# One list-scheduled order for all engines, PSUM banks by class, batch 0 mixed pair by pair, and the tails of all batches as a ninth MLP block

## The chip, the cores and the metric

One core of a Trainium2 chip. The metric is the time of one execution on the device, in microseconds (us), as the median of several runs. A run is called fast or slow by its time and its granted matrix-engine clock. PE is the matrix engine (PEld its weight loads), ACT the scalar engine, DVE the vector engine, POOL the GpSimd engine, SP the sync engine, which here only issues DMAs. POOL issues the loads that also cast from f32 to bf16; SP issues plain loads, stores and DMA transposes.

## The reference

Random-feature attention for 8 batches of 8 heads, then a mixer. In short:

```python
def _attn_ref(q, k, v, omega):              # q, k, v: 8 x 8 x 576 x 64, omega: 128 x 64
    phi = lambda x: concat(cos(x @ omega.T), sin(x @ omega.T)) / sqrt(128)
    kv  = einsum('bhsm,bhsd->bhmd', phi(k), v)
    z   = sum(phi(k), axis=2)
    num = einsum('bhsm,bhmd->bhsd', phi(q), kv)
    den = einsum('bhsm,bhm->bhs', phi(q), z)     # kept away from 0
    return num / den

def _moe_ref(x, U, V, w_ch1, w_ch2):        # x: 8 x 576 x 512, w_ch1: 512 x 2048, w_ch2: 2048 x 512
    h = x.transpose(0, 2, 1) @ U @ V        # token mixing of rank 32
    u = x + h.transpose(0, 2, 1)
    return u + maximum(u @ w_ch1, 0) @ w_ch2
```

The kernel works by head pair (32 of them, four to a batch). A *quad* is the k, q and v of four heads, so two quads to a batch: quads 0 and 1 are batch 0, quads 2 and 3 batch 1. Of a batch's 576 tokens 512 make four full tiles; the other 64 are its *tail*. In the code and the traces kraw and qraw are a quad's k and q as loaded, kT and qT their transposes; x is the attention's result, u the token-mixed x, and uT its transpose, which the MLP's first matmuls (W1, from w_ch1) read; W2 is w_ch2. *Mixing* is the way from x to u.

## The kernel before

It lets a framework schedule instructions written in a loop of steps: in step `s` one quarter of an MLP block (two batches behind), the angles of head pair `s` and the attention of pair `s - 1`. All matmul outputs share two rotating sets of PSUM buffers, `"at"` and `"mm"`.

```python
    def angles(g):                                   # head pair g
        pk = psum.tile([P, 2, 512], F32, name="pk", tag="at")
        ...                                          # 8 matmuls, then DVE scales to int32 "ang"
        for a in range(2):
            nc.scalar.activation(out=ft[:, 0, a, :], in_=low[:, a, :, 0], func=ACT.Sin, scale=TO_RAD)
            nc.gpsimd.tensor_scalar(out=ang[:, a, :], in0=ang[:, a, :], scalar1=TURN / 4.0,
                                    scalar2=1.0, op0=ALU.add, op1=ALU.mult)      # a quarter turn: cosine next
        for a in range(2):
            nc.scalar.activation(out=ft[:, 1, a, :], in_=low[:, a, :, 0], func=ACT.Sin, scale=TO_RAD)
    ...
    def channel_in(b, fs):                           # W1 groups of batch b
        for f0 in fs[::2]:
            h_ps = psum.tile([P, 2, SM], F32, name="h_ps", tag="mm")
            for f in range(2):
                for ct in range(NCT):
                    nc.tensor.matmul(h_ps[:, f, :], w1(ct, f0 + f), uT[:, :, ct, :],
                                     start=(ct == 0), stop=(ct == NCT - 1))
                nc.scalar.activation(out=hid[:, f0 + f, :], in_=h_ps[:, f, :], func=ACT.Relu)
    ...                                              # channel_in_tail: after every second batch, 64 matmuls of 128 columns
    for s in range(NG + 6):
        if s >= 6:
            b, mc = divmod(s - 6, 4)
            if b < B:
                mlp_chunk(b, mc)
        n = s // 2 + 1
        if s % 2 == 0 and 4 <= n < NG // 2:
            load_quad(n); load_v(n); transpose_quad(n); widen_v(n)
        ...
        if s < NG:
            angles(s)
        ...                                          # weights: W1 from step 3 on, W2 in steps 4 and 5
        if s != 4:
            attend(s - 1)
```

Of the kernel before, what the change touches and what calls it, by code (L numbers as in the profile page):

```python
# [30 lines left out]
HALF = M * 9  # L31


# [3 lines left out]

# [3 lines left out]


SYNC = mybir.DependencyInfo(mybir.DependencyClass.Sync, mybir.DependencyReason.DATA)
# [3 lines left out]
def kernel(  # L47
# [23 lines left out]
    hidp = ctx.enter_context(tc.tile_pool(name="hidp", bufs=1))  # L71
    outp = ctx.enter_context(tc.tile_pool(name="outp", bufs=3))
    smallp = ctx.enter_context(tc.tile_pool(name="smallp", bufs=4))
    psum = ctx.enter_context(tc.tile_pool(name="psum", bufs=2, space=bass.MemoryType.PSUM))


    ident = const.tile([P, P], BF16, name="ident")
    om_f = stage.tile([P, 2, D], F32, name="om_f")
    nc.sync.dma_start(om_f, omega.unsqueeze(1).to_broadcast([P, 2, D]))
    warm = stage.tile([P, 1], F32, name="warm")  # L80
    nc.vector.memset(warm, 0.0)
    nc.scalar.activation(out=warm, in_=warm, func=ACT.Sin)
    WT = const.tile([P, M], BF16, name="WT")

    def omega_t():
        om_b = stage.tile([P, 2, D], BF16, name="om_b")
        nc.vector.tensor_copy(om_b, om_f)
        wt_ps = psum.tile([P, P], BF16, name="wt_ps", tag="at")
        nc.tensor.transpose(wt_ps, om_b, ident)
        nc.vector.tensor_copy(WT, wt_ps)  # L90

# [3 lines left out]
    U_f = stage.tile([P, NT + 1, R], F32, name="U_f")  # L95
    Vf = stage.tile([P, S], F32, name="Vf")

    def load_low_rank():
        U9 = moe_U.rearrange("(p s) r -> p s r", s=NS)
        for g in range(4):  # L100
            ordered(nc.sync.dma_start(Vf[g * R:(g + 1) * R, :], moe_V))
        for e in range(2):
            r = slice(e * TL, (e + 1) * TL)
            ordered(nc.sync.dma_start(U_f[r, 0:NT, :], U9[:, e:2 * NT:2, :]))
            ordered(nc.sync.dma_start(U_f[r, NT, :], U9[:, 8, :]))

    def cast_low_rank():
        ordered(nc.gpsimd.tensor_copy(Ub, U_f[:, 0:NT, :]))
        ordered(nc.gpsimd.tensor_copy(Ut, U_f[:, NT, :]))
        ordered(nc.gpsimd.tensor_copy(Vb.rearrange("r (s p) -> r s p", p=TL), Vf.rearrange("r (p s) -> r s p", s=NS)))  # L110

    W1b = const.tile([P, 4, NCT, 512], BF16, name="W1b")
    W2b = const.tile([P, NFT, C], BF16, name="W2b")

    def load_w1(a):
        return nc.gpsimd.dma_start(W1b[:, a, :, :],
                                   moe_w_ch1[:, a * 512:(a + 1) * 512].rearrange("(c p) f -> p c f", p=P))

    def load_w2(a):
        return nc.gpsimd.dma_start(W2b[:, 4 * a:4 * a + 4, :],  # L120
                                   moe_w_ch2[a * 512:(a + 1) * 512, :].rearrange("(f p) c -> p f c", p=P))

    def w1(ct, f):
        return W1b[:, f // 4, ct, f % 4 * P:(f % 4 + 1) * P]

    NV = 4
    vq = []
    for i in range(NV):
        a = const.tile([P, 2 * NS, D + 1], BF16, name=f"vq{i}")
        nc.vector.memset(a[:, :, D:D + 1], 1.0)  # L130
        vq.append(a)

    def ordered(ins):
        return tc.keep_in_program_order(ins)


    raw, tpos = {}, {}
# [5 lines left out]
    def load_quad(n, parts=1):  # L143
        for name in ("k", "q"):
            raw[name, n] = rawp.tile([P, 2, NS * D], BF16, name=f"{name}raw")
        for i in range(parts):
            w = slice(i * 2 // parts, (i + 1) * 2 // parts)
            for name, src in (("k", k), ("q", q)):
                last = ordered(nc.gpsimd.dma_start(raw[name, n][:, w, :], quad(src, n)[:, w, :]))
        return last  # L150

    def load_v(n):
        raw["v", n] = rawp.tile([P, 2, NS * D], F32, name="vraw")
        return ordered(nc.sync.dma_start(raw["v", n], quad(v, n)))

    def widen_v(n):
        ordered(nc.gpsimd.tensor_copy(vq[n % NV][:, :, 0:D],
                                      raw.pop(("v", n)).rearrange("p i (s d) -> p (i s) d", d=D)))

    def transpose_quad(n):  # L160
        for name in ("k", "q"):
            tpos[name, n] = tposp.tile([P, NS, P], BF16, name=f"{name}T")
            last = ordered(nc.sync.dma_start_transpose(tpos[name, n], raw.pop((name, n)).rearrange("p i e -> p (i e)")))  # L163
        return last

    def transpose_first():
        for name in ("k", "q"):
            tpos[name, 0] = tposp.tile([P, NS, P], BF16, name=f"{name}T")
        for blocks in (range(0, 4), range(4, NS)):
            t_ps = psum.tile([P, 2, 8, P], BF16, name="t_ps", tag="mm")  # L170
            for j, (name, copy) in enumerate((("k", nc.vector.tensor_copy), ("q", nc.scalar.copy))):
                src = raw[name, 0].rearrange("p i e -> p (i e)")
                for c in blocks:
                    nc.tensor.transpose(t_ps[:, j, c - blocks[0], :], src[:, c * P:(c + 1) * P], ident)
                copy(out=tpos[name, 0][:, blocks[0]:blocks[-1] + 1, :], in_=t_ps[:, j, 0:len(blocks), :])


    st, x_of = {}, {}

    def angles(g):  # L180
        n, i = divmod(g, 2)
        kT, qT = tpos["k", n], tpos["q", n]

        ang = angp.tile([P, 2, HALF], I32, name="ang")

        def units(dst, src):
            nc.vector.tensor_scalar(out=dst, in0=src, scalar1=TO_UNITS, scalar2=None, op0=ALU.mult)  # L187

        def at(s):
            f = NS * i + s  # L190
            return slice((f % 2) * D, (f % 2 + 1) * D), f // 2

        pk = psum.tile([P, 2, 512], F32, name="pk", tag="at")
        for j in range(4):
            for e in range(2):
                r, c = at(2 * j + e)
                nc.tensor.matmul(pk[:, e, j * P:(j + 1) * P], kT[r, c, :], WT[r, :])  # L197
        units(ang[:, 0, 0:1024], pk.rearrange("p e c -> p (e c)"))
        pt = psum.tile([P, 2, M], F32, name="pt", tag="at")
        r, c = at(8)  # L200
        nc.tensor.matmul(pt[:, 0, :], kT[r, c, :], WT[r, :])
        nc.tensor.matmul(pt[:, 1, :], WT[r, :], qT[r, c, :])  # L202
        units(ang.rearrange("p a c -> p (a c)")[:, 1024:1280], pt.rearrange("p a c -> p (a c)"))
        pq = psum.tile([P, 2, 512], F32, name="pq", tag="at")
        for e in range(2):
            r, c = at(e)
            nc.tensor.matmul(pq[:, e, :], WT[r, :], qT[r, c:c + 4, :])  # L207
        units(ang[:, 1, P:HALF].rearrange("m (t e p) -> m e t p", e=2, p=TL),
              pq.rearrange("m e (t p) -> m e t p", p=TL))

        ft = featp.tile([P, 2, 2, HALF], BF16, name="ft")
        low = ang.rearrange("p a c -> p (a c)").bitcast(I16).rearrange(
            "p (a c e) -> p a c e", a=2, e=2)
        for a in range(2):
            nc.scalar.activation(out=ft[:, 0, a, :], in_=low[:, a, :, 0], func=ACT.Sin, scale=TO_RAD)  # L215
            nc.gpsimd.tensor_scalar(out=ang[:, a, :], in0=ang[:, a, :], scalar1=TURN / 4.0,  # L216
                                    scalar2=1.0, op0=ALU.add, op1=ALU.mult)
        for a in range(2):
            nc.scalar.activation(out=ft[:, 1, a, :], in_=low[:, a, :, 0], func=ACT.Sin, scale=TO_RAD)  # L219
        st[g] = ft  # L220

    def key_values(g):
        n, i = divmod(g, 2)
        ft = st[g]
        kv_ps = psum.tile([P, 2, 512], F32, name="kv_ps", tag="mm" if g < 4 else "at")
        for f in range(2):
            o = slice(f * (D + 1), (f + 1) * (D + 1))
            for s in range(NS):
                c = (s % 2 * 4 + s // 2) * M if s < 8 else 1024
                for hh in range(2):  # L230
                    r = slice(hh * TL, (hh + 1) * TL)
                    nc.tensor.matmul(kv_ps[:, hh, o], ft[r, f, 0, c:c + M], vq[n % NV][r, NS * i + s, :],  # L232
                                     start=(s == 0), stop=(s == NS - 1))
        kvb = kvp.tile([P, 2, 2, D + 1], BF16, name="kvb")
        nc.vector.tensor_copy(kvb.rearrange("p h f d -> p h (f d)"), kv_ps[:, :, 0:2 * (D + 1)])  # L235
        st[g] = (ft, kvb)

    def numerators(g):
        b, hp = divmod(g, 4)
        ft, kvb = st.pop(g)  # L240
        if hp == 0:
            x_of[b] = xp.tile([P, NT, C], BF16, name="x")
            if b % 2 == 0:
# [139 lines left out]
    def mlp_chunk(b, mc):  # L383
# [4 lines left out]
        elif mc == 2:  # L388
            channel_out(b, (0, 1))
            if b % 2 == 1:  # L390
                channel_in_tail(b // 2)
# [102 lines left out]
```

## Time and profile before

| | before |
|---|---|
| median of 3 runs | 428.71 us (428.13 to 429.35) |
| profiled span | 426.5 us |
| PE busy | 363.9 us, 85% |
| first W1 matmul | 47.2 us |
| a pair of batches in the middle | 98.0 and 96.4 us |

Of the profile page of the kernel before, the span, PE's busy line, and the rows of 40 equal slices (10.66 us each; a digit is tenths busy, or tenths of full clock):

```profile
span 426.5 us, 8510 instructions
...
PE 363.9 (85%) x3639; PEld 186.5 (44%) x3639; DVE 198.4 (47%) x335; ACT 226.3 (53%) x278; POOL 122.9 (29%) x131
...
PE   3364988978899979978899989978899989979995
...
PEclk9996899999999999989999999999999999999999
DMA  8989998578247581677439483498438320133013
```

PE is lightly used in the first four slices and shows a rhythm of dips after that. The DMA engines are near full only for some 80 us.

The same page, three of the costliest groups (line, engine, operation, out<-in, shapes, count | busy us, mean ns | idle before it, and what ended it):

```profile
L339 PE MATMUL h_ps<-uT,W1b 128*128 128x512 bf16 x512 | 122.6, 379 | 14.3 <-ACT hid L341 12.8
L364 PE MATMUL ch_ps<-W2b,hid 128*128 128x512 bf16 x512 | 123.3, 383 | 5.1 <-DVE o L367 3.9
L254 PE MATMUL nd<-kvb,ft 128*128 128x65 bf16 x512 | 23.0, 198 | 7.5 <-DVE kvb L235 7.2
```

W1 groups wait 12.8 us in all for ACT's relu to free their buffer. In the page's chain of waits PE has just over half:

```profile
PE 53%; ACT 19%; DVE 9%; POOL 7%; issue 6%; DMA 3%; SPq 2%; POOLq 0%; ACTq 0%; DVEq 0%
```

Busy time by stretch (stretch, its length, then busy us of each engine with counts, granted clock, DMA share of 16 engines, GB/s). A share adds up the packets' times, so packets in flight together can bring it over 1:

```profile
0.00:40.00 40.00, 18.48 (x303) 13.51 (x303) 20.57 (x41) 22.89 (x23) 22.36 (x31) 0.94 0.93 169
40.00:80.00 40.00, 34.26 (x336) 16.66 (x337) 21.78 (x37) 25.22 (x33) 19.14 (x21) 0.93 1.03 176
80.00:115.00 35.00, 29.96 (x308) 14.55 (x306) 18.82 (x31) 20.65 (x25) 10.54 (x10) 1.00 0.64 128
115.00:380.00 265.00, 242.46 (x2471) 122.66 (x2471) 131.31 (x219) 145.57 (x180) 70.89 (x69) 0.99 0.52 97
101.60:199.60 98.00, 89.36 (x900) 44.80 (x900) 48.84 (x82) 55.61 (x69) 28.48 (x29) 0.98 0.57 110
199.60:296.00 96.40, 87.68 (x901) 44.37 (x900) 48.87 (x82) 55.57 (x69) 28.44 (x28) 1.00 0.63 111
```

One line of PE's timeline gives the true price of a matmul: 64 of them in a row, no gap.

```profile
385.39 14.06 PE L339 MATMUL h_ps<-uT,W1b 128*128 128x512 bf16 x64
```

The group's mean is 379 ns, but a start comes every 217 ns (13.89 us of the chain for 64). Records overlap, so work is counted in starts.

### The profile page before, as it was taken

Reading aid. Unit: us, or ns where it says so; the run is one execution under the profiler, and the core shown is the slowest. Engines: PE = TensorE matmul, PEld = TensorE weight load, DVE = VectorE, ACT = ScalarE, POOL = GpSimd, SP = SyncE. Lnnn points to the kernel's source line nnn. Section 1 sums busy time; section 2 is a strip of 40 time slices with the busy share of each in tenths; the row PEclk is TensorE's granted clock in tenths of the full one; section 3 lists DMA queues with packets and bytes.
Section 4 is the critical chain, followed back from the end, with each engine's and each line's share of the span. In section 5 each row is a group of like instructions: output and inputs, shape, how many; then the busy total and the mean of one; then the engine's idle time right before and its main releaser. Section 6 shows DMA issues by size and latency. Waiting matters only on the chain.

```text
span 426.5 us, 8510 instructions
## 1 busy us (share of the span) xinstructions
PE 363.9 (85%) x3639; PEld 186.5 (44%) x3639; DVE 198.4 (47%) x335; ACT 226.3 (53%) x278; POOL 122.9 (29%) x131
## 2 busy tenths in 40 slices
PE   3364988978899979978899989978899989979995
PEld 2253444434455434434456444434456444434452
DVE  2566663564535643664435552674434561550011
ACT  2667598327835196626845197626855187405320
POOL 5366583123323060423232051424233031200000
PEclk9996899999999999989999999999999999999999
DMA  8989998578247581677439483498438320133013
GB/s 134 180 172 208 192 192 146 106 178 170 36 81 137 120 155 18 111 172 155 59 56 162 84 170 39 81 174 174 68 40 178 75 50 2 26 70 68 9 41 74
DMA packets 76533, 46.54 MB, mean 109 GB/s; under 512 B 55376, under 2 KB 67664, under 8 KB 76496
## 3 DMA queue, kind: packets, MB, share of 16 engines
q1 hardware_dynamic: 63536, 32.37, 36.6%
q0 software_dynamic: 12960, 13.63, 21.2%
q8 instruction: 28, 0.46, 0.5%
q14 instruction: 9, 0.07, 0.0%
HBM read 37.14 MB, written 9.44 MB: 109 GB/s over the span
## 4 chain that ended last, share of the span: by engine, by line
PE 53%; ACT 19%; DVE 9%; POOL 7%; issue 6%; DMA 3%; SPq 2%; POOLq 0%; ACTq 0%; DVEq 0%
PE ch_ps L364 23%; PE h_ps L339 15%; ACT ft L215 7%; ACT ft L219 7%; POOL ang L216 6%; DVE ang L187 4%; ACT hid L341 4%; PE ch_ps L376 3%; PE ht_ps L352 3%; PE nd L254 2%; SPq L163 2%; DVE u L313 2%; DMA kraw<-in_k_dram 1%; PE hn L312 1%; DMA vraw<-in_v_dram 1%
## 5 line engine op out<-in xcount | busy, mean ns | idle before, releaser
L339 PE MATMUL h_ps<-uT,W1b 128*128 128x512 bf16 x512 | 122.6, 379 | 14.3 <-ACT hid L341 12.8
L216 POOL TENSOR_SCALAR ang<-ang 128x1152 int32<-128x1152 int32 x64 | 73.3, 1148 | 211.7 <-ACT ft L215 211.2
L364 PE MATMUL ch_ps<-W2b,hid 128*128 128x512 bf16 x512 | 123.3, 383 | 5.1 <-DVE o L367 3.9
L341 ACT ACTIVATE hid<-h_ps 128x512 bf16<-128x512 f32 x128 | 73.3, 592 | 66.0 <-PE h_ps L339 65.8
L215 ACT ACTIVATE ft<-ang 128x1152 bf16<-128x1152 int16 x64 | 74.0, 1159 | 40.9 <-DVE ang L187 39.6
L219 ACT ACTIVATE ft<-ang 128x1152 bf16<-128x1152 int16 x64 | 74.1, 1160 | 40.3 <-POOL ang L216 40.0
L339 PEld LDWEIGHTS <-W1b 128*128 128x128 bf16 x512 | 46.9, 97 | 64.9 <-issue 15.7
L364 PEld LDWEIGHTS <-hid 128*128 128x128 bf16 x512 | 47.3, 98 | 58.7 <-issue 9.6
L367 DVE TENSOR_TENSOR o<-ch_ps,u 128x512 f32<-128x512 f32 x32 | 22.1, 690 | 82.6 <-PE ch_ps L364 78.6
L187 DVE TENSOR_SCALAR ang<-pk 128x1024 int32<-128x1024 f32 x32 | 39.0, 1220 | 32.5 <-PE pt L202 25.6
L187 DVE TENSOR_SCALAR ang<-pq 128x1024 int32<-128x1024 f32 x32 | 39.1, 1221 | 17.9 <-PE pq L207 17.7
L232 PEld LDWEIGHTS <-ft 64*128 64x128 bf16 x1152 | 24.1, 98 | 19.8 <-issue 8.1
L254 PE MATMUL nd<-kvb,ft 128*128 128x65 bf16 x512 | 23.0, 198 | 7.5 <-DVE kvb L235 7.2
L254 PEld LDWEIGHTS <-ft 128*128 128x128 bf16 x512 | 21.4, 100 | 18.0 <-issue 8.7
L354 ACT ACTIVATE hidt<-ht_ps 128x512 bf16<-128x512 f32 x16 | 9.5, 592 | 28.0 <-PE ht_ps L352 28.0
L235 DVE CAST kvb<-kv_ps 128x260 bf16<-128x260 f32 x32 | 13.5, 422 | 21.3 <-PE kv_ps L232 21.3
L267 DVE TENSOR_TENSOR x<-nd,rec 128x512 bf16<-128x512 f32 x32 | 22.1, 692 | 1.1
L313 DVE TENSOR_TENSOR u<-hn,x 128x1024 bf16<-128x1024 f32 x16 | 18.8, 1219 | 5.0 <-PE hn L312 5.0
L265 DVE RECIPROCAL nd<-nd 128x10 f32<-128x10 f32 x32 | 7.3, 228 | 29.5 <-PE nd L260 29.4
L187 DVE TENSOR_SCALAR ang<-pt 128x256 int32<-128x256 f32 x32 | 13.3, 417 | 14.4 <-PE pt L202 14.1
L352 PE MATMUL ht_ps<-utT,W1b 128*128 128x128 bf16 x256 | 16.9, 219 | 3.5 <-ACT hidt L354 3.5
L197 PE MATMUL pk<-WT,kT 64*128 64x128 bf16 x256 | 15.7, 232 | 4.8 <-DMA kT<-kraw 2.5
(69 smaller groups left out, 251.0 us busy)
## 6 DMA issues: line engine op xcount, KB each, us to landing
vraw<-in_v_dram SPq DMA_DIRECT2D x16, 576.0 KB, 4.3
out_dram<-o SPq DMA_DIRECT2D x72, 128.0 KB, 2.4
kraw<-in_k_dram POOLq DMA_DIRECT2D x15, 288.0 KB, 4.2
qraw<-in_q_dram POOLq DMA_DIRECT2D x15, 288.0 KB, 5.9
W1b<-in_moe_w_ch_dram POOLq DMA_DIRECT2D x4, 512.0 KB, 8.1
W2b<-in_moe_w_ch_dram POOLq DMA_DIRECT2D x4, 512.0 KB, 11.1
kraw<-in_k_dram POOLq DMA_DIRECT2D x2, 144.0 KB, 4.1
qraw<-in_q_dram POOLq DMA_DIRECT2D x2, 144.0 KB, 4.3
```

What stands on the lines that cost most here:

```text
L187: nc.vector.tensor_scalar(out=dst, in0=src, scalar1=TO_UNITS, scalar2=None, op0=ALU.mult)
L215: nc.scalar.activation(out=ft[:, 0, a, :], in_=low[:, a, :, 0], func=ACT.Sin, scale=TO_RAD)
L216: nc.gpsimd.tensor_scalar(out=ang[:, a, :], in0=ang[:, a, :], scalar1=TURN / 4.0, scalar2=1.0, op0=ALU.add, op1=ALU.mult)
L219: nc.scalar.activation(out=ft[:, 1, a, :], in_=low[:, a, :, 0], func=ACT.Sin, scale=TO_RAD)
L232: nc.tensor.matmul(kv_ps[:, hh, o], ft[r, f, 0, c:c + M], vq[n % NV][r, NS * i + s, :], start=(s == 0), stop=(s == NS - 1))
L254: nc.tensor.matmul(nd[:, t // 2, 2 * (t % 2) + hh, :], ft[:, f, 1, c:c + P], kvb[:, hh, f, :], start=(f == 0), stop=(f == 1))
L267: nc.vector.tensor_tensor(out=x[:, :, hp * P:(hp + 1) * P].rearrange("p (a t) (h d) -> p a t h d", a=2, h=2), in0=nd[:, :, 0:4, 0:D], in1= ...
L313: nc.vector.tensor_tensor(out=u[:, 2 * a:2 * a + 2, :], in0=h_ps, in1=x[:, 2 * a:2 * a + 2, :], op=ALU.add)
L339: nc.tensor.matmul(h_ps[:, f, :], w1(ct, f0 + f), uT[:, :, ct, :], start=(ct == 0), stop=(ct == NCT - 1))
L341: nc.scalar.activation(out=hid[:, f0 + f, :], in_=h_ps[:, f, :], func=ACT.Relu)
L352: nc.tensor.matmul(h_ps[:, a, f, :], w1(ct, f0 + 4 * a + f), utT[:, ct, :], start=(ct == 0), stop=(ct == NCT - 1))
L364: nc.tensor.matmul(ch_ps, hid[:, f, t * P:(t + 1) * P], W2b[:, f, :], start=(f == 0), stop=(f == NFT - 1))
```

## The change

The kernel now carries its own planner. Each piece of work is an `Op` with an engine, a cost, what it needs, a rank, and for PE the PSUM banks it may take. The planner picks, again and again, the op that can start earliest (rank breaks ties), with a rough model of transfers, and the kernel then emits all instructions in that order, which nothing reorders. The starts of the engines' lists are fixed by hand. Banks are split by class: angles and mixing (0, 1), key-values and numerators (4, 5), small things (6), MLP (7, 2, 3). W1 groups of batch b are ranked to alternate with W2 quarters of batch b - 1. Batch 0 is mixed head pair by head pair. The eight tails become a ninth block of 512 columns at the end.

```diff
-    psum = ctx.enter_context(tc.tile_pool(name="psum", bufs=2, space=bass.MemoryType.PSUM))
+    psum = ctx.enter_context(tc.tile_pool(name="psum", bufs=1, space=bass.MemoryType.PSUM))
+    ps = psum.tile([P, 8, 512], F32, name="ps")
 ...
+    def add(self, name, engine, cost, emit, needs=(), rank=0, takes=None, frees=(), kb=0, rate=390.0, slack=0.0, queue=None):
 ...
+    def order(self):
+        while waiting:
+            for o in waiting:
+                if o.behind not in begun or any(n not in done for n in o.needs):
+                    continue
+                at = max([free[o.engine]] + [done[n] + o.slack for n in o.needs if ...])
+                ...                                   # and the earliest free bank of o.takes
+                key = (at, o.rank)
+                if best is None or key < best[0]:
+                    best = (key, o, place)
+            ...
+            if o.kb:                                  # a transfer: when it will have landed
+                begin = max(end + 0.9, line.get(q, 0.0))
+                need = o.kb / o.rate
+                shared = min(max(other - begin, 0.0), 2 * need)
+                line[q] = begin + need + shared / 2
+                done[o.name] = line[q] + 0.9
 ...
+    BY_PE = (0,)                                      # quads transposed by PE; all others by a DMA transpose:
+    NRAW = 2
+                add(("tp", name, n), SP, 1.3, tpd, needs=[("ld", name, n)] + old, kb=295, rate=200.0, rank=0.4)
 ...
+    for p in range(4):                                # batch 0: mixing by head pair
+        add(("hu0", p), PE, 0.25, ..., needs=[("x", p), "lowc"], takes=SM1, rank=(0, p, 5))
+        add(("ut0", p), PE, 0.5, ut0, needs=[("huc0", p)], takes=SM1, rank=(0, p, 6))
 ...
+    MM = [(7,), (2,), (3,)]
+    for b in range(B + 1):                            # b == TAIL: the ninth block
+            add(("w1", b, f), PE, 0.867, w1, ..., takes=MM, rank=(1, b * 32 + 2 * f, 0), slack=0.1)
+            add(("r", b, f), SCA, 0.55, relu, ...)
+                add(("w2", b, t, j), PE, 0.867, w2, ..., rank=(1, (b + 1) * 32 + 8 * t + 2 * j + 1, 0), slack=0.1)
 ...
+    plan.line(POOL, ["ident", ("ld", "k", 0), ..., ("pk", 2), ("wv", 1), ("W1", 1), ("pq", 2), ("pk", 3), ("pq", 3)])
+    plan.line(SP, [("first", "k"), ("ldv", 0), ("tp", "k", 1), ("tp", "q", 1), ("ldv", 1), ("tp", "k", 2), ("tp", "q", 2), ("ldv", 2)])
+    order = plan.order()
+    with tc.manual_schedule():
+        for o in order:
+            o.emit()
-    for s in range(NG + 6):
-        ...
```

## The prediction

> **What bounds the kernel now.** The matrix engine, with gaps. The page shows PE busy 363.9 of 426.5 us. The Trainium skill ("Trainium Kernel Development and Optimization", section "Performance Expectations") warns that matmul busy time misleads because matmuls are pipelined. The trace agrees: a 512-column matmul is recorded as 379 ns, but from 385.5 to 399.4 us 64 of them take 13.89 us, 217 ns each. So I count starts in the timeline: an MLP block of 128 such matmuls costs 27.75 us; a head pair's angles, key-values and numerators 2.02 us; token mixing 1.75 us a batch; a batch-pair tail 7 us. Sum: 8x27.75 + 32x2.02 + 8x1.75 + 4x7 + 3 = 332 us. About 95 us are lost:
> - Start: MLP matmuls run only after 40 us. Sines start at 11.5 us, with holes until 25 us. The queues' share is 0.8 to 1.25 until 70 us; granted clock 0.72 to 0.77 from 30 to 50 us.
> - Middle: a pair of batches takes 98.0 and 96.4 us against 83 us of PE work. The chain of waits runs through angles, sine, quarter turn, sine; PE's waits are MLP groups behind ACT (12.8 us) and nd behind the kvb cast (7.2 us).
> - End: about 5 us.
>
> **What the change does.** It removes little: the ninth block costs 27.75 us where four tails cost 28; sines, relus, evictions and loads stay. It moves: (a) PE order: W1 groups of batch b alternate with W2 quarters of b-1, so relus arrive evenly; (b) PSUM by class: three MLP banks that angle evictions never hold; (c) attention enters when its inputs are planned to be ready; (d) batch 0: first half quad as f32 on two hardware queues, mixing by head pair, so the first MLP starts earlier; (e) tails come last.
>
> **Cost and path.** ACT needs 148 us of sines and about 85 of relus, DVE about 205, POOL about 125: none binds, so the steady state should be PE-bound: a pair falls from 97 to about 78 us (75 of work plus 4% of waits). The 7 us of tails moves to the end. The start is bounded by queues: q, k, v of batch 0 and half of batch 1 (5.3 MB), W1 (4.2 MB) and transposes must arrive; before moved 134 to 208 GB/s there. I expect the first MLP matmul near 35 us, but W1's last parts and batch 1's u only near 50 and 65 us, so PE has holes until 65 us. By then it has done 38 us; 294 remain, times 1.035 is 304, plus 4 for the end: about 370.
>
> **Prediction: 370 us, 8 in 10 between 354 and 388.** Faster by over 2%: 0.95; within 2%: 0.03; slower: 0.02.
>
> **What would show it.** PE's slices at 9 tenths from 65 us to the end; PE busy near 350 us, over 93% of the span; W1 groups waiting under 5 us in total for the relu; the chain over 75% PE; first W1 matmul at 33 to 38 us; remaining PE idle mostly before 65 us, behind DMA; the last 14 us one pure W2 block. Counts of sines and relus nearly unchanged.
>
> **What would make it wrong.** Low: queues deliver faster, W1 is there by 40 us and the holes vanish (355). High: the plan assumes durations and transfers; if a load or transpose is late, all in-order engines stall together, or weight loads delay k and q of batch 1 (385 or more).

## The result, and the profile after

| | before | after | predicted |
|---|---|---|---|
| median | 429.03 us (428.13 to 429.52, 4 runs) | 407.5 us (406.2 to 408.5, 4 runs) | 370 (354 to 388) |
| ratio of fast runs, 95% interval | | 0.9499 (0.9471 to 0.9527) | |
| profiled span | 426.5 us | 404.4 us | |
| first W1 matmul | 47.2 us | 41.4 us | 33 to 38 |
| last W1 part, last W2 part landed | 55.9, 66.7 us | 51.0, 81.7 us | near 50, not stated |
| uT of batch 1 issued, landed | 90.5, 94.8 us | 107.7, 114.5 us | u near 65 |

A ratio is the mean time of one kernel's fast runs over that of the other's fast runs of the same rounds, so it is not quite the ratio of the medians.

The change is faster by 5%, a good third of what was predicted. The same lines of the page after:

```profile
span 404.4 us, 8121 instructions
...
PE 358.1 (89%) x3416; PEld 176.3 (44%) x3462; DVE 199.4 (49%) x340; ACT 225.7 (56%) x280; POOL 123.1 (30%) x132
...
PE   3266769689679999999999999999999999999995
...
PEclk9998769879959999999999999999999999999999
DMA  8999999999999787799744141023115121111223
```

From the thirteenth slice on (about 121 us) PE is full to the end; the stretches below show it nearly full from 115 us. Before that it is emptier than it was, its clock dips, and the DMA engines are full all the way. Three of the groups show that PE's wait for relu is gone; that for the cast, 7.2 us before, is 1.0 us by the list of waits (here every PSUM bank has the tile name `ps`):

```profile
L561 PE MATMUL ps<-W2b,hid 128*128 128x512 bf16 x537 | 140.1, 383 | 7.1 <-issue 3.4
L548 PE MATMUL ps<-uT,W1b 128*128 128x512 bf16 x512 | 134.5, 389 | 2.8 <-DMA uT<-u 2.5
L408 PE MATMUL ps<-kvb,ft 128*128 128x65 bf16 x512 | 23.2, 198 | 6.1 <-ACT ft L380 5.1
```

(39 of the 576 W2 records are missing from this trace; counts below allow for it.) The chain, and the stretches:

```profile
PE 77%; DMA 11%; DVE 4%; issue 3%; POOL 2%; ACT 2%; POOLq 0%
```

```profile
0.00:40.00 40.00, 19.23 (x341) 14.05 (x346) 21.98 (x49) 23.10 (x25) 26.85 (x39) 0.97 1.05 186
40.00:80.00 40.00, 31.07 (x301) 14.62 (x303) 21.40 (x32) 22.85 (x29) 15.92 (x19) 0.84 1.24 202
80.00:115.00 35.00, 26.54 (x367) 13.90 (x372) 24.34 (x43) 21.00 (x19) 17.97 (x18) 0.84 1.18 202
115.00:380.00 265.00, 261.51 (x2325) 124.95 (x2358) 128.21 (x212) 156.35 (x204) 62.35 (x59) 0.99 0.44 86
```

From 115 to 380 us PE is busy 261.5 of 265 us, against 242.5 before. In the first 115 us it is busy 76.8 us, against 82.7.

Counting starts shows the same in work. By 115 us the kernel before had started 120 W1 and 64 W2 matmuls (184 x 0.217 = 39.9 us) and ten head pairs (20.2 us). The kernel after had done block 0 and hardly more (about 130 x 0.217 = 28.2 us) and eleven pairs (22.2 us). So it is about 10 us of work *behind* at 115 us, and then finishes in 289 us against 311: it gains some 32 us in the steady part and gives back 10 in the start.

The chain of waits in order of time shows what the start waits for (start, us, what):

```profile
37.62 13.99 DMA kT<-kraw
...
69.18 12.49 DMA W2b<-in_moe_w_ch_dram
...
107.74 6.72 DMA uT<-u
114.51 1.87 PE ps L548 x4
```

A transpose of quad 3's k takes 14 us to land; the last W2 part takes 12.5; batch 1's u is transposed only at 107.7. At 114.5 us comes the first W1 matmul of batch 1, after which PE is full.

Around 40 us, POOL's and then SP's timeline (start, us, what, [idle before <- what ended it]):

```profile
39.96 0.78 POOL L244 DMA_DIRECT2D W2b<-in_moe_w_ch_dram  x1
52.17 0.70 POOL L280 DMA_DIRECT2D kraw<-in_k_dram  x1 [11.43 <-DMA kT<-kraw]
52.90 1.06 POOL L384 TENSOR_SCALAR ang<-ang 128x1024 int32<-128x1024 int32 x1
```

```profile
37.62 10.44 SPq L316 DMA_TRANSPOSE kT<-kraw  x2
48.16 0.53 SPq L285 DMA_DIRECT2D vraw<-in_v_dram  x1
48.80 7.50 SPq L316 DMA_TRANSPOSE qT<-qraw  x2
```

POOL stands 11.43 us in front of a load whose buffer is still being read by that slow transpose, and the quarter turn behind it, which ACT needs, waits too. The Trainium skill, "TensorE: Matmul & The Clock Gate", the table at the head of the page, says that ScalarE, VectorE and GpSimdE have strict first-in, first-out queues; these lines agree. SP is held 10.44 us by two transposes, the k of quads 3 and 4 (the second alone 7.60 us, though its data had landed at 38.9), so the q of quad 3, whose load had landed at 41.6 us, is sent to its transpose at 48.8.

### The profile page after: what moved, and what is told of

It reads as the page before. It is cut to its first block, busy times and chain, and to the rows that moved or that the text cites. A ratio compares the mean times of both kernels' runs of the same rounds, so it can differ in the third digit from the quotient of the medians.

```text
span 404.4 us, 8121 instructions
## 1 busy us (share of the span) xinstructions
PE 358.1 (89%) x3416; PEld 176.3 (44%) x3462; DVE 199.4 (49%) x340; ACT 225.7 (56%) x280; POOL 123.1 (30%) x132
## 3 DMA queue, kind: packets, MB, share of 16 engines
q1 hardware_dynamic: 62512, 32.22, 39.9%
## 4 chain that ended last, share of the span: by engine, by line
PE 77%; DMA 11%; DVE 4%; issue 3%; POOL 2%; ACT 2%; POOLq 0%
PE ps L548 31%; PE ps L561 29%; PE ps L394 4%; PE ps L408 4%; DMA kT<-kraw 3%; DMA W2b<-in_moe_w_ch_dram 3%; PE ps L351 2%; DMA qraw<-in_q_dram 2%; PE ps L370 2%; POOL ang L384 2%; DMA uT<-u 2%; ACT ft L380 2%; DVE ang L329 1%; PE ps L512 1%; PE ps L413 1%
## 5 line engine op out<-in xcount | busy, mean ns | idle before, releaser
L380 ACT ACTIVATE ft<-ang 128x1024 bf16<-128x1024 int16 (+2 forms) x130 | 144.0, 1142 | 40.1 <-POOL ang L384 24.6
L553 ACT ACTIVATE hid<-ps 128x512 bf16<-128x512 f32 x144 | 85.5, 595 | 112.5 <-PE ps L548 111.9
L561 PE MATMUL ps<-W2b,hid 128*128 128x512 bf16 x537 | 140.1, 383 | 7.1 <-issue 3.4
L548 PE MATMUL ps<-uT,W1b 128*128 128x512 bf16 x512 | 134.5, 389 | 2.8 <-DMA uT<-u 2.5
L329 DVE TENSOR_SCALAR ang<-ps 128x1024 int32<-128x1024 f32 (+2 forms) x97 | 89.4, 943 | 43.3 <-PE ps L351 13.3
L384 POOL TENSOR_SCALAR ang<-ang 128x1280 int32<-128x1280 int32 (+1 forms) x64 | 73.6, 1153 | 97.3 <-ACT ft L380 96.8
L548 PEld LDWEIGHTS <-W1b 128*128 128x128 bf16 x576 | 53.2, 99 | 65.7 <-issue 8.5
L561 PEld LDWEIGHTS <-hid 128*128 128x128 bf16 x576 | 52.4, 98 | 65.2 <-issue 7.7
L573 DVE TENSOR_TENSOR o<-ps,u 128x512 f32<-128x512 f32 x32 | 22.1, 690 | 94.7 <-PE ps L561 91.4
L394 PE MATMUL ps<-vq,ft 64*128 64x65 bf16 x1152 | 28.8, 198 | 1.9 <-ACT ft L380 0.9
L408 PE MATMUL ps<-kvb,ft 128*128 128x65 bf16 x512 | 23.2, 198 | 6.1 <-ACT ft L380 5.1
L425 DVE TENSOR_TENSOR x<-ps,rec 128x512 bf16<-128x512 f32 x32 | 22.1, 692 | 1.1
L280 POOL DMA_DIRECT2D kraw<-in_k_dram x15 | 10.9, 727 | 35.3 <-DMA kT<-kraw 35.2
L398 DVE CAST kvb<-ps 128x260 bf16<-128x260 f32 x32 | 13.6, 424 | 12.2 <-PE ps L394 12.0
```

What stands on the lines that cost most here:

```text
L329: nc.vector.tensor_scalar(out=dst, in0=src, scalar1=TO_UNITS, scalar2=None, op0=ALU.mult)
L380: nc.scalar.activation(out=held["ft", g].rearrange("p f a c -> p f (a c)")[:, f, lo:hi], in_=low[:, lo:hi, 0], func=ACT.Sin, scale=TO_RAD)
L384: nc.gpsimd.tensor_scalar(out=ang, in0=ang, scalar1=TURN / 4.0, scalar2=1.0, op0=ALU.add, op1=ALU.mult)
L394: nc.tensor.matmul(kv_ps[:, hh, o], ft[r, f, 0, c:c + M], vq[n % NV][r, NS * (g % 2) + s, :], start=(s == 0), stop=(s == NS - 1))
L408: nc.tensor.matmul(nd[:, t // 2, 2 * (t % 2) + hh, :], ft[:, f, 1, c:c + P], kvb[:, hh, f, :], start=(f == 0), stop=(f == 1))
L425: nc.vector.tensor_tensor(out=x[:, :, hp * P:(hp + 1) * P].rearrange("p (a t) (h d) -> p a t h d", a=2, h=2), in0=nd[:, :, 0:4, 0:D], in1= ...
```

## The experiments

A regularity came out of the first runs and serves all the others: **in this plan's order, the profiled span is the time of batch 1's first W1 matmul plus 289 us.** The last column, the rest, is the span minus that start. Where it grows, the work after batch 1's start has paid for starting earlier. The times in us come from each run's profile (s: slow, not leaned on):

| label | median us | ratio to before (95%) | W2 all there | x of pair 7 | batch 1's first W1 | rest |
|---|---|---|---|---|---|---|
| the change | 407.5 | 0.950 (0.947-0.953) | 81.7 | 90.9 | 114.5 | 289.9 |
| again | 408.6 | 0.956 (0.948-0.963) | 85.2 | 94.0 | 117.0 | 290.0 |
| w_quarter (wrong result) | 393.8 | 0.919 (0.915-0.923) | 68.9 | 81.3 | 102.5 | 289.9 |
| t_plain (wrong result) | 392.9 | 0.916 (0.913-0.919) | 72.4 | 82.3 | 102.3 | 288.9 |
| both (wrong result) | 384.5 | 0.898 (0.895-0.900) | 63.4 | 73.5 | 93.4 | 289.0 |
| rates | 406.6 | 0.946 (0.940-0.951) | 92.6 | 92.5 | 122.5 | 287.3 s |
| raw3 | 405.1 | 0.947 (0.943-0.951) | 81.2 | 88.9 | 110.7 | 289.2 |
| mix4 | 404.8 | 0.944 (0.940-0.948) | 83.0 | 92.1 | 104.8 | 298.6 |
| mix6 | 408.8 | 0.951 (0.945-0.956) | 84.9 | 93.8 | 113.7 | 294.0 |
| hold | 401.6 | 0.937 (0.932-0.942) | 68.1 | 85.2 | 104.0 | 296.5 |
| early3 | 403.2 | 0.936 (0.926-0.947) | 77.0 | 85.7 | 109.3 | 289.0 |
| early3_hold | 401.6 | 0.926 (0.917-0.934) | 77.7 | 87.2 | 110.6 | 292.9 s |
| early3_hold_mix | 404.2 | 0.927 (0.918-0.936) | 82.7 | 94.7 | 113.2 | 294.2 s |
| phase | 406.8 | 0.945 (0.940-0.950) | 82.8 | 92.0 | 115.2 | 289.4 |
| early3_raw3 | 405.3 | 0.946 (0.942-0.949) | 76.6 | 87.5 | 114.4 | 288.9 |
| early3_raw3_hold | 403.0 | 0.939 (0.934-0.944) | 80.7 | 93.8 | 114.3 | 292.3 s |
| early3_raw3_plan | 407.5 | 0.952 (0.945-0.958) | 90.8 | 95.0 | 113.3 | 290.4 |
| pe3 | 403.7 | 0.942 (0.938-0.946) | 79.4 | 90.8 | 110.2 | 291.1 |
| pe3_hold | 406.2 | 0.947 (0.944-0.950) | 65.7 | 83.5 | 114.6 | 290.0 |

Kernels sent together ran on one chip, with the kernel before beside them, so the ratios are the safer comparison between groups. The changed kernel itself reads 0.950 on one chip and 0.956 on another (`again`): differences of half a per cent between groups are not read. The medians take in slow runs, the ratios do not.

Two theories stood at first. **T**: the start is bound by what the queues carry. **O**: the queues could carry it, but the fixed order puts engines in line behind late data.

### Less to carry: w_quarter, t_plain, both

```diff
# w_quarter: same order; a quarter of each weight part is loaded and used four times
-        nc.gpsimd.dma_start(W1b[:, a, :, :], moe_w_ch1[:, a * 512:(a + 1) * 512].rearrange("(c p) f -> p c f", p=P))
+        nc.gpsimd.dma_start(W1b[:, a, 0, :], moe_w_ch1[0:P, a * 512:(a + 1) * 512])
-        nc.gpsimd.dma_start(W2b[:, 4 * a:4 * a + 4, :], moe_w_ch2[a * 512:(a + 1) * 512, :].rearrange("(f p) c -> p f c", p=P))
+        nc.gpsimd.dma_start(W2b[:, 4 * a, :], moe_w_ch2[a * 512:a * 512 + P, :])
# t_plain: same order; plain copies of the same bytes
-                    nc.sync.dma_start_transpose(transposed(name, n), held.pop((name, n)).rearrange("p i e -> p (i e)"))
+                    nc.sync.dma_start(transposed(name, n), held.pop((name, n)).rearrange("p i e -> p (i e)").rearrange("p (c s) -> p c s", s=P))
```

All three give a wrong result on purpose. `both` has both edits.

> Wrong result on purpose: each of the eight weight loads brings a quarter of its bytes (the matmuls reuse that quarter), the instruction order is that of the changed kernel. Theory T (the start is bound by what the queues can carry): 6.3 of 8.4 MB gone, at the 190 GB/s seen there 33 us of queue time, so 375 to 388 us, the last W2 part landing by 55 us instead of 81.7, batch 1's first W1 matmul near 85 to 95 us instead of 114.5. Theory O (the fixed order blocks the engines, the bytes are secondary): over 399 us.

> Wrong result on purpose: the 30 DMA transposes of k and q become plain copies of the same bytes between the same tiles, order unchanged. If the transposes' slow passage through the queues is what starves the start: 380 to 395 us. If the bytes of the loads are: within 5 us of 407. Theory O gives a gain only as far as POOL's and PE's waits for kT and qT (35 and 11 us before 115 us) shrink.

> Wrong result on purpose: quarter weights and plain copies together, order unchanged. Each alone gained about 13 us (393.8 and 392.9). If both feed one shared limit (what the queues carry), together they bring the transfers near the plan's and the time near the plan's own end of 361 plus some 8 us for the finish and steady waits: 365 to 378 us. If a wait outside the queues (the order) sets the start by now: 386 to 393 us.

Measured: 393.8, 392.9 and 384.5 us. Taking away three quarters of the weights' bytes, or the transposing of the transposes, each brings batch 1's first W1 matmul forward by 12 us, and together by 21; the rest stays 289. Transfers are a cause, shown, and the two starts add up almost fully (21 of 24 us). `t_plain` is within its forecast. But `w_quarter` fell short of T's forecast (375 to 388), and `both` of its own (365 to 378): with most of the load gone, batch 1's MLP still starts only at 93.4 us. What is left there is in good part the order itself. The planner's own table, with its fast transfers, puts that start at 84.7 us and the end of the plan at 360.8.

The stretch from 40 to 80 us, first of `t_plain`, then of `both`:

```profile
40.00:80.00 40.00, 33.96 (x339) 15.01 (x338) 23.79 (x36) 26.97 (x34) 21.41 (x23) 0.91 1.16 260
```

```profile
40.00:80.00 40.00, 38.33 (x435) 18.22 (x439) 30.06 (x50) 34.40 (x41) 27.41 (x30) 1.00 1.01 240
```

Without transposing, the same full queues move 260 GB/s where the changed kernel moved 202 (the line of that stretch above; from 40 to 115 us it is 228 against 202). The pages' DMA lines, of the change and then of `t_plain`, show that the same bytes now travel in far fewer packets; whether the packets or the transposing itself cost the time, no run separates:

```profile
DMA packets 75930, 46.90 MB, mean 116 GB/s; under 512 B 54644, under 2 KB 66804, under 8 KB 75892
```

```profile
DMA packets 44730, 46.89 MB, mean 120 GB/s; under 512 B 19604, under 2 KB 31764, under 8 KB 44692
```

The SP instruction, too, is quicker: a kT copy occupies SP 0.46 to 1.65 us, a kT transpose 1.27 to 7.60. The kernel before makes the same 30 transposes of k and q, but with fewer transfers at a time: its DMA share from 80 to 115 us is 0.64, against 1.18.

### Planning with slower transfers: rates

```diff
-    def add(self, ..., kb=0, rate=390.0, slack=0.0,
+    def add(self, ..., kb=0, rate=300.0, slack=0.0,
-                ... kb=295, rate=200.0, rank=0.4)            # k, q transposes; u's and tails' likewise
+                ... kb=295, rate=100.0, rank=0.4)
-        add(("ak", g), PE, 0.27, ak, needs=kmain + ["WT"], ...
+        add(("ak", g), PE, 0.27, ak, needs=kmain + ["WT"] + ([("aq", g - 1)] if 3 <= g < 8 else []), ...
```

> Correct result: the planner is told slower transfers (300 instead of 390 bytes per ns, transposes 100 instead of 200), which puts its landings of W1 and W2 at 47 and 73 us (the changed kernel's trace: 51.0 and 81.7; its own plan: 39.6 and 57.9); an order angle-q before the next angle-k is added so that it finds a plan. Theory O (the plan was made for transfers that do not come): 387 to 398 us. Theory T: 402 to 412 us.

Measured: 406.6 us (fast runs 402.9 to 407.2), no better. Slower rates in the plan do not help: the loads are issued later still (quad 3's k at 37.3 us instead of 33.3), and W2, planned at 73, lands at 92.6 us (in a slow profile). As even this plan was too fast, the run does not settle what a plan with true rates would give.

### No waiting of POOL for a raw buffer: raw3

```diff
-            held[name, n] = rawp.tile([P, 2, NS * D], BF16, name=f"{name}raw")
+            held[name, n] = rawp.tile([P, 2, NS * D], BF16, name=f"{name}raw", bufs=3)
# om_f and om_b move into xtail, which is written much later, to make room
```

> Correct result: a third buffer for each of kraw and qraw, order unchanged, so that POOL's load instructions no longer wait for the transpose two quads back (35 us of waits in 8 places) and the quarter turns behind them go on time. If this in-line blocking is the cost: 392 to 402 us, POOL's wait for kT under 8 us. Theory T: within 3 us of 407, or slower, because loads start earlier and crowd the queues more.

Measured: 405.1 us. POOL's wait for kT fell from 35.2 to 5.7 us as expected, and the median by 2.4 us, with ratio intervals that overlap. The forecast of 392 to 402 is missed: the wait was real, but W2 is there no earlier (81.2 us) and x of pair 7 only 2 us earlier.

### Batch 1's mixing ahead of batch 2's attention: mix4, mix6

In the change, x of pair 7, the last of batch 1, is there at 90.9 us, yet uT is issued at 107.7.

```diff
# mix4 (mix6: batches 1 to 6, from the next batch's third pair on)
-        add(("ak", g), PE, 0.27, ak, needs=kmain + ["WT"], ...
+        add(("ak", g), PE, 0.27, ak, needs=kmain + ["WT"] + ([("aq", g - 1)] if g >= 5 else [])
+            + ([("hn", 1, 1), ("hnt", 1)] if g == 8 else []), ...
# and at(g) after ak(g), at(g - 1); aq(g) after ak(g), from g = 5 on
```

> Correct result: the planner must put batch 1's mixing ahead of the angles of head pairs 8 and later (and keep the angle instructions in one order). In the changed kernel x of head pair 7 is there at 91 us, but batch 1's uT is issued only at 107.7 us because PE and DVE first take, in line, attention of batch 2 that waits for late transposes. If that blocking is the cost: uT of batch 1 issued within 10 us of x of pair 7, and 390 to 399 us. If batch 1's attention itself is too late (queues): 402 to 410 us.

> Correct result: a softer form of the same, for batches 1 to 6: each batch's mixing before the angles of the next batch's third head pair. The plan's own end is the lowest of the variants (358 against 361). Theory order: 393 to 402 us; theory queues: 402 to 410 us.

Measured: 404.8 and 408.8 us; the ratio intervals of both overlap that of the change. In `mix4` uT is issued 7.9 us after x of pair 7 instead of 16.8, and batch 1's MLP starts 10 us earlier. But the rest grows from 290 to 298.6 us, and x of pair 11 (batch 2's last) comes at 137.5 instead of 121.2: the wait looks moved to the next batch. `mix6` is the same as the change within the scatter.

### Later quads held back: hold

```diff
-                    needs=need + ([("ld", name, n - 2)] if n > 1 else []), kb=590, rank=0.2 + 0.1 * j)
+                    needs=need + ([("ld", name, n - 2)] if n > 1 else []) + ([("W2", 3)] if n == 4 else []), ...
-        add(("ldv", n), ..., needs=need + ([("ldv", n - 1)] if n else []), ...
+        add(("ldv", n), ..., needs=need + ([("ldv", n - 1)] if n else []) + ([("W2", 3)] if n == 4 else []), ...
# and ak, at, aq kept in order as in mix4
```

> Correct result: the planner issues the loads of quads 4 and later (batch 2 on) only after the last W2 part is planned to have landed. If early prefetch of later batches crowds out W2 and batch 1's transposes: W2 complete by 68 us instead of 81.7, and 388 to 399 us. If the queues were needed for those loads anyway, because batch 2's attention is then the late part: 402 to 412 us.

Measured: 401.6 us, ratio 0.937, with an interval that lies below that of the change. W2 is complete at 68.1 us, as forecast, and batch 1's MLP starts at 104.0. Of those 10.5 us, 6.6 are paid back (rest 296.5). The gain is 6 us, where 8 to 19 were expected. Holding the quads back brings W2 forward by 13.6 us; that the time gained comes from it is not shown, because the run also fixes the order of the angles, which was never run alone, and because `pe3_hold` below has W2 as early and no such gain.

### Quad 3 first: early3, early3_hold, early3_hold_mix

```diff
-                     ("pq", 0), ("pk", 1), "lowc", ("pq", 1), ("pk", 2), ("wv", 1), ("W1", 1), ("pq", 2), ...
+                     ("pq", 0), ("pk", 1), "lowc", ("pq", 1), ("pk", 2), ("ld", "k", 3), ("ld", "q", 3), ("wv", 1), ("W1", 1), ...
-    plan.line(SP, [..., ("tp", "k", 2), ("tp", "q", 2), ("ldv", 2)])
+    plan.line(SP, [..., ("tp", "k", 2), ("tp", "q", 2), ("ldv", 2), ("tp", "k", 3), ("tp", "q", 3)])
```

`early3_hold` adds the edit of `hold`; `early3_hold_mix` also puts batch 1's mixing ahead of pair 9's angles.

> Correct result: only two fixed lists change. POOL issues the k and q loads of quad 3 (the second half of batch 1) right after the quarter turn of head pair 2, about 22 us, ahead of the second W1 part, instead of at 33 us with 2 quads and 3 weight parts at once; SP transposes them before anything of quad 4. In the changed kernel the transposes of quad 3 land at 51.6 (k) and 61.0 us (q) and x of head pair 7 is ready at 91. If the lateness of quad 3 is what starts batch 1's MLP late: qT of quad 3 lands by 42 us, x of pair 7 by 78, first W1 matmul of batch 1 by 102, and by the rule end = that start + 289 us, 385 to 393 us. If the queues' total is the limit: x of pair 7 after 87 us and 402 us or more.

> Correct result: the same, and quads 4 and later are loaded only after the last W2 part is planned to land. Expected by theory order: first W1 matmul of batch 1 by 97 us and 380 to 390 us; if hold only moves the lack to batch 2 (as in hold, whose rest was 296 instead of 289 us): 388 to 396 us.

> Correct result: the same, and batch 1's mixing goes ahead of the angles of head pair 9. Expected: uT of batch 1 issued within 10 us of x of pair 7; 378 to 390 us if the earlier start isn't paid back in batch 2, 390 to 398 if it is.

Measured: `early3` 403.2 us. Quad 3's kT lands at 40.3 us instead of 51.6, qT at 48.6 instead of 61.0, and still x of pair 7 comes only 5 us earlier. Its timeline shows why:

```profile
49.15 0.73 POOL L280 DMA_DIRECT2D qraw<-in_q_dram  x1 [6.36 <-DMA qT<-qraw]
49.89 1.16 POOL L287 CAST vq<-vraw 128x1152 bf16<-128x1152 f32 x1
51.01 1.04 POOL L384 TENSOR_SCALAR ang<-ang 128x1024 int32<-128x1024 int32 x1
51.10 1.18 PE L394 MATMUL ps<-vq,ft 64*128 64x65 bf16 x36 [9.80 <-POOL vq L287]
```

Now POOL stands before a load of quad 5, and PE waits 9.80 us for the v cast in line behind it. `early3_hold` and `early3_hold_mix` have two fast runs of four each (397.6 and 399.4; 398.9 and 399.2): about 1% under `hold` at best. Their forecasts of 380 to 390 and 378 to 390 are missed.

### Quad 3 first and three raw buffers: again, early3_raw3, early3_raw3_hold, early3_raw3_plan

The edits of `early3` and `raw3` together; with `hold`; or with `NRAW = 3` told to the planner and the angle order fixed. `again` is the changed kernel on the same chip.

> Control: the changed kernel itself, on the chip of the three below: 404 to 409 us, first W1 matmul of batch 1 at 112 to 117 us.

> Correct result: early3 (quad 3 loaded and transposed first) plus raw3 (three raw buffers for k and q). In early3 POOL stood 4.2 and 6.4 us (36.6 to 49.2 us) in front of loads of quad 5 that waited for quad 3's transposes, PE waited 9.8 us for the v cast behind them, and x of head pair 7 was ready at 85.7 us. If what is left of the cause is this in-line blocking on POOL: x of pair 7 by 77 us, first W1 matmul of batch 1 by 99 us, end at that start + 289, so 386 to 392 us. If the transfers themselves are the rest: x of pair 7 at 83 or later and 397 us or more.

> Correct result: the same with quads 4 and later loaded after the last W2 part is planned to land. If crowding by later quads matters once nothing blocks in line: x of pair 7 by 73 us and 382 to 391 us; if it only moves the lack to batch 2: 390 to 398 us.

> Correct result: as early3_raw3, with the planner told of the third raw buffer and the angle instructions kept in one order (its own end 359.6 against 361.2 us). Loads of quad 5 are then placed earlier on POOL: if transfers are the rest, this crowds them more and is slower than early3_raw3 by 2 us or more; if in-line waits are, faster by 1 to 4 us.

Measured: 408.6, 405.3, 403.0 and 407.5 us. `early3_raw3` (0.946) is no better than `early3` (0.936) or `raw3` (0.947) alone; only with `hold` (0.939) does the group clearly beat its control, `again` (0.956). The wait has moved to SP, where one transpose of a batch 2 quad holds the queue 9.95 us:

```profile
43.99 9.95 SPq L316 DMA_TRANSPOSE qT<-qraw  x1
54.03 0.53 SPq L285 DMA_DIRECT2D vraw<-in_v_dram  x1
```

The load behind it is the v of quad 3; its cast ends at 69.6 us, and pair 6, which needs it, is normalised at 78.4. The numbers meet the second reading of the expectation (x of pair 7 at 87.5, over 397 us), but they don't show that transfers alone are the rest: what the trace shows is again a wait in line, now SP's behind a slow transpose. `early3_raw3_plan` was to be slower than `early3_raw3` by 2 us or more; it is, by 2.2, but the intervals overlap.

### Quad 3 transposed by PE: pe3, pe3_hold

```diff
-    BY_PE = (0,)
+    BY_PE = (0, 3)
# and ak, at, aq kept in order as in mix4; pe3_hold adds hold
```

> Correct result: quad 3 (second half of batch 1) is transposed by PE, as quad 0 is, with DVE and ACT copies, instead of by two DMA transposes that land 14 and 12 us after their issue at 37.6 and 48.8 us; the angle instructions are kept in one order. If the transposes' slow passage through full queues holds back batch 1: both raw loads of quad 3 land by 42 us, so its angles can start by 45 instead of 61, x of head pair 7 by 82 us, first W1 matmul of batch 1 by 104 us and 392 to 398 us. If only the total carried counts (2 of 30 transposes are taken away): 404 us or more.

> Correct result: the same with quads 4 and later loaded after the last W2 part is planned to land. Expected: W2 complete by 68 us, first W1 matmul of batch 1 by 100 us, rest 289 to 296, so 389 to 397 us; 400 or more if batch 2 pays it back.

Measured: 403.7 and 406.2 us in 5 rounds. `pe3` gains about 1% over the change, not the 2 to 4% expected, and x of pair 7 doesn't move. The next transpose in line, of quad 4, takes the place of quad 3's in the wait:

```profile
54.46 1.41 POOL L280 DMA_DIRECT2D kraw<-in_k_dram  x2 [11.91 <-DMA kT<-kraw]
```

`pe3_hold` missed its forecast of 389 to 397: W2 is there at 65.7 us and x of pair 7 at 83.5, both earlier than in any other correct variant, yet batch 1's MLP starts at 114.6 as in the change. Its u is ready at 97.9, its transpose is issued at 104.2, holds SP 8.24 us and leads to the first W1 matmul only 10.4 us after its issue. Early data alone is thus not enough.

### Is the alternation what fills the steady part? phase

```diff
-                rank=(1, b * 32 + 2 * f, 0), slack=0.1)                                 # W1 groups
+                rank=(1, b * 64 + 2 * f, 0), slack=0.1)
-                ... rank=(1, (b + 1) * 32 + 8 * t + 2 * j + 1, 0), slack=0.1)           # W2 quarters
+                ... rank=(1, b * 64 + 32 + 8 * t + 2 * j + 1, 0), slack=0.1)
```

> Correct result: only the ranks of MLP work change, so that a batch's 16 W1 groups come before its W2 quarters and before the next batch's W1, instead of alternating with the W2 quarters of the batch before. If the alternation is what lets ACT keep up with the relus: the rest after batch 1's first W1 matmul grows from 289 to over 296 us and W1 groups wait for relus by over 5 us more in total. If three MLP banks and a list-scheduled order are enough: within 4 us of 407.

The edit did what it says: in its trace W1 and W2 take turns in whole blocks, 18 stretches in all, against 226 in the change. Measured: 406.8 us, rest 289.4: nothing changes. W1 and W2 may follow one another in blocks; the alternation is not what keeps PE full. Whether the separate banks do it, or the order, or attention running further ahead (x of the last pair at 289.6 us against 376.0 before), no run here separates.

## Why the prediction was wrong

**The step that failed** is this one: "I expect the first MLP matmul near 35 us, but W1's last parts and batch 1's u only near 50 and 65 us, so PE has holes until 65 us. By then it has done 38 us; 294 remain". The first MLP matmul came at 41.4 and W1's last part at 51.0, close enough. But batch 1's u was ready at 106.4 us (the end of the second u addition) and transposed at 114.5, and until then PE had holes. By 114.5 us PE had done about 54 us of work (block 0 27.75, eleven pairs 22.2, two mixings 3.5). The start so lost 60 us, where 65 - 38 = 27 were allowed: 33 us too few, of an error of 37.

**What was mis-sized in it.**
- *The list of what must arrive.* It counted q, k, v of three quads, W1 and "transposes", without a duration for the transposes, left out W2's 4.2 MB, and did not ask what the planner would prefetch. It also left out quad 3, though batch 1's u needs it: the transposes of its k and q landed only at 51.6 and 61.0 us. The Trainium skill, "Trainium Kernel Development and Optimization", section "Key Constraints", says that DMAs issued from SP, ACT and POOL all run on the same 16 engines and interleave. The trace agrees: in the changed kernel a kT transpose lands 7.5 us after its issue in the median and 17.0 at most, against 5.1 and 9.0 before, with the same bytes; and in `w_quarter`, where only POOL's loads shrink, the longest of these transposes on SP falls to 11.7. `both` takes 21 us out of the start. Shown. The landing lines of kT, before and after:

```profile
DMA to landing us min/median/max: 3.3/5.1/9.0
```

```profile
DMA to landing us min/median/max: 3.2/7.5/17.0
```

- *What the order does with late data.* 93.4 us in `both`, and 84.7 in the plan itself, are still far from 65. The plan's own table has x of pair 7 ready at 65.2 us but uT issued at 78.8. Likewise batch 1's attention is ready at 73.5 us in `both`, and uT goes out 14.7 us later, behind batch 2's attention. `mix4` shows that this gap can be narrowed (7.9 us) but that the rest then grows by 9. The prediction named the danger, "if a load or transpose is late, all in-order engines stall together", gave it 385 us or more, and set its upper bound at 388, too low.
- *The clock.* The Trainium skill, "TensorE: Matmul & The Clock Gate", section "Part 1: The HAM clock gate (the 'warmup' mystery)", says that the array runs at half rate by default and after an idle window, and at full rate only while kept busy. The trace agrees: at 114.51 us, after the wait, four W1 matmuls take 1.87 us of the chain; from 119.8 us on most such groups take 0.87 to 1.03. The granted clock is 0.59 from 114 to 121 us and 1.00 from 121 to 200. From 40 to 115 us it is 0.84, where the kernel before had 0.93 and 1.00 (40 to 80, 80 to 115 us). Holes thus cost more than their length: an estimate from these numbers is 0.16 x 75 = 12 us at most, as PE was not always at work then. It was not in the sum.

**What was right.** "It removes little" and "the steady state should be PE-bound": after 114.5 us some 277 us of work (331 in all - 54) took 285 us up to the last matmuls, 3% over, where 3.5% was predicted. W1 groups wait 2.8 us in total (under 5 predicted), none of it for a relu in the page's line. The chain is 77% PE (over 75 predicted). The last 14 us are one pure W2 block. PE busy, 358 us, is near the 350 named, but 89% of a longer span. For the reason (a), that alternating W1 and W2 spreads the relus, `phase` shows no effect: the forecast of the steady part was right and this reason for it was not.

**What stays open.** Thirteen variants with a correct result that change the start gained up to some 9 us, most of them under 5. Removing the raw-buffer wait, bringing quad 3 forward, or moving its transposes to PE each exposed the next wait in line. Some order that starts batch 1 near 90 us without making batch 2 late may exist; none was found. How batch 1's late start (114.5 us, with u forecast near 65) divides between transfers and order is only bounded: `both` takes off 21 us, and the transfers that it leaves may still cost some. Which part of the change fills the steady part is not separated either.

**A version that beats both kernels** is `hold`: a correct result, 401.6 us, 0.937 of before (0.932 to 0.942) against 0.950 for the change (0.947 to 0.953). `early3_hold` has a lower ratio, 0.926, but from two fast runs of four.

## What to carry to other kernels

When a schedule is made denser, ask first what must arrive before its dense part can begin, and price that list with the landing times of the trace under the load to come, not with rates from a quiet stretch: here the steady part gained 32 us and the start gave 10 back. A fixed order of all engines turns one late transfer into a wait on every in-order queue, and removing a single such wait shows the next one; look for load to take off the queues (`both`, a wrong result and so only a bound: 23 us) before shuffling the order (up to 9 us). Test the reason given for a gain by itself: the alternation was forecast to matter, and without it the time was the same.

## What the Trainium skill lacked or had wrong

- "DMA: Bandwidth & Descriptors", section "Latency and other measured facts", gives a transpose an effective bandwidth of 261 GB/s, or 350 to 400 when contiguous. It gives no rate for transposes among other traffic. Here a 288 KB transpose landed 3.2 us after its issue at best, 7.5 in the median and 17.0 at most, and with plain copies in their place the same queues moved 260 instead of 202 GB/s from 40 to 80 us.
- No page gives the time for which a transpose holds the issuing queue while other transfers run (the DMA page has only cycles of the sequencer without the transfer, for earlier chips as a group). SP was occupied 1.27 to 7.60 us by one kT transpose, 0.46 to 1.65 us by a plain copy of the same bytes, and what stood behind it waited.
